# FFN weight sums made beside the float64 conversion and read back from DRAM, a group's second transposes moved three products on, first FFN products issued sooner

## The chip, the cores and the metric

One core of a Trainium2 chip runs the whole program in one launch. The metric is the device time of an execution in microseconds (us); less is better. The engines are named as the profile names them: PE (matrix multiply; PEld is its weight load), DVE (vector), ACT (scalar), POOL (GpSimd), SP (the engine that issues most DMAs here). Each engine runs its own instructions in program order and waits at semaphores for the others.

## The reference

Three stages follow each other, all in float32: an attention with exponential features, a mixture of eight experts with one expert for each token, and a dense feed-forward layer (FFN) with three parallel first matrices.

```python
def phi(x):
    proj = np.einsum('bhsd,df->bhsf', x, w_phi)
    proj = proj - np.max(np.abs(proj), axis=-1, keepdims=True)
    return np.concatenate([np.exp(proj), np.exp(-proj)], axis=-1)
q_p, k_p = phi(q), phi(k)                          # 8 batches, 8 heads, 576 tokens
kv = np.einsum('bhsf,bhsd->bhfd', k_p, v); z = np.sum(k_p, axis=2)
num = np.einsum('bhsf,bhfd->bhsd', q_p, kv)
x = num / (np.einsum('bhsf,bhf->bhs', q_p, z)[..., None] + 1e-06)   # -> (4608, 512)

do_compute = x @ w_skip > 0                        # the other tokens pass unchanged
e_idx = np.argmax(xc @ w_gate, axis=1)             # xc: the tokens computed
y[mask] = gate_w[mask, None] * (np.maximum(xc[mask] @ w1[e], 0) @ w2[e])
x[do_compute] = xc + y

h = np.maximum(np.maximum(x @ w1, x @ w2), x @ w3) # 512 -> 768, three matrices
out = h @ w_out                                    # 768 -> 512
```

## The kernel before

**Precision.** A float32 operand of a large product is split into a high part, made by a copy on ACT, and a low part, made by a subtraction on DVE. A product is then three matmuls (`mm3`, L483 to L485). A "split" below is such a pair of one ACT and one DVE instruction, 512 or 256 columns wide. The same lines, L795 and L796, do it for weights (tiles `w`, `wB`, `wC`) and for the FFN's input (tiles `xB`, `xT`).

**Attention** takes the first 360 us or so. Beside it runs `conv`, a generator that turns the 24 FFN weight tiles from float64 bits into float32: a load `pf`, four DVE steps and two ACT squares or copies `sq`, two POOL instructions (L202, L203), and a DMA of the result `da` to the DRAM tensor `wfd`. One of its steps is taken in each of 60 attention iterations, the rest by `pump`.

**Experts.** Blocks of up to three token tiles go through layer 1 and layer 2. `pump` stands after each part of a layer and does three things: it splits one or two expert weight tiles (`w_split`, loads five splits ahead by `w_dma`), or, when those are done, takes a step of `w1_prep`, and then a step of `conv`. POOL also issues the gathers of tokens (`xg`), the scatters of results (`xb<-y`, L966) and the index lists (L301). SP issues the loads `stg<-in_w_exp` and the stores to `wfd` in one order.

**FFN.** Each of the products is done by a seven-product scheme in place of eight: from the four quarters of an operand (x11, x12, x21, x22) four sums are made, and seven products of quarters or sums give the result. `Quad.step(p)` issues product p (six matmuls in layer 1). Products 1, 6, 5 and 3 accumulate in one PSUM tile, and after 1, 6 and 5 ACT copies the running value out (`pu`, L1124) before the next of them may start. DVE adds the results (L1109, L1111, L1112, L1134).

The 4608 tokens go in nine groups of 512. A group has nine quads in layer 1 (nine pairs of weight tiles) and two in layer 2. All groups do layer 1 first. `do(n, at, f)` hangs a piece of side work behind product `at` of quad n, in the order 6, 4, 1, 5, 7, 2, 3.

For its input a group needs two times eight transposes on PE (`f_xt`, L1060) into two PSUM tiles of the pool `ps_t` (`tp`), which then feed the splits `x_put` and the sums `x_sums` (DVE, L1075). The two halves (i = 0 and 1) use the same two PSUM tiles, one half after the other, so that the second half's transposes wait for the last read of the first half. `x_next` puts the halves at quads n0+5 and n0+6.

The weights of layer 1 come from `w1_steps`: for each of nine pairs it loads both tiles of `wfd` into one staging tile `stg` (four of them, shared with the expert loads and with `f_load`), makes four sums on POOL (`sc`, L799 to L802), and splits one half tile, one tile and two pairs of sums. The first three pairs are split during the last expert block, the others beside the first group's first quads, five steps a pair.

At the start of the FFN the first group's transposes, splits and sums are written out in full ahead of the first product.

Of the kernel before, what the change touches and what calls it, by code (L numbers as in the profile page):

```python
# [19 lines left out]
P = 128  # L20
# [25 lines left out]
def kernel(  # L46
# [43 lines left out]
    wfd = dram.tile([NFT, P, 512], F32, name="wfd")  # L90

# [89 lines left out]
    def from_double(t, pool, i):  # L181
# [23 lines left out]
        yield  # L205
        nc.sync.dma_start(out=wfd[i], in_=af)

    conv_done = [0]

    def conv_steps(pool):  # L210
        def start(i):
            t = pool.tile([P, 1024], I32, name="pf")
            nc.sync.dma_start(out=t, in_=w_ffn[i].bitcast(I32))
            return t

        nxt = start(0)
# [552 lines left out]
    sc_p = ctx.enter_context(tc.tile_pool(name="sc", bufs=2))  # L769
# [28 lines left out]
    def sums_left(sc, x11, x12, x21, x22, eng):  # L798
        eng.tensor_tensor(out=sc[:, 2], in0=x21, in1=x22, op=ALU.add)  # L799
        eng.tensor_tensor(out=sc[:, 0], in0=sc[:, 2], in1=x11, op=ALU.subtract)  # L800
        eng.tensor_tensor(out=sc[:, 1], in0=x11, in1=x21, op=ALU.subtract)
        eng.tensor_tensor(out=sc[:, 3], in0=x12, in1=sc[:, 0], op=ALU.subtract)  # L802

    def sums_right(sc, x11, x12, x21, x22, eng):
        eng.tensor_tensor(out=sc[:, 2], in0=x12, in1=x11, op=ALU.subtract)
        eng.tensor_tensor(out=sc[:, 0], in0=x22, in1=sc[:, 2], op=ALU.subtract)
        eng.tensor_tensor(out=sc[:, 1], in0=x22, in1=x12, op=ALU.subtract)
        eng.tensor_tensor(out=sc[:, 3], in0=x21, in1=sc[:, 0], op=ALU.subtract)

# [12 lines left out]
    class Operands:  # L822


        def __init__(self, raw, side, whole, half, sums, eng=nc.vector):
            self.raw, self.side, self.whole, self.half, self.pool, self.eng = raw, side, whole, half, sums, eng
            self.blocks = {}

        def steps(self):
            return [self.sums, self.single, self.wide, lambda: self.pair(0), lambda: self.pair(2)]  # L830

        def sums(self):
            r = self.raw
            x = [[r[:, a, b * 256 : (b + 1) * 256] for b in range(2)] for a in range(2)]
            self.sc = self.pool.tile([P, 4, 256], F32, name="sc")
            if self.side == "rows":
                sums_left(self.sc, x[0][0], x[0][1], x[1][0], x[1][1], nc.gpsimd)
            elif self.side == "cols":
                sums_left(self.sc, x[0][0], x[1][0], x[0][1], x[1][1], nc.gpsimd)
            else:  # L840
                sums_right(self.sc, x[0][0], x[0][1], x[1][0], x[1][1], nc.gpsimd)

        def single(self):
            h = self.half()
            rows = self.side == "rows"
            split(h, self.raw[:, 1, 256:] if rows else self.raw[:, 0, 0:256], self.eng)
            self.blocks[4 if rows else 1] = h

        def wide(self):
            w = self.whole()  # L850
            split(w, self.raw[:, 0 if self.side == "rows" else 1], self.eng)
            a, b = {"rows": (1, 2), "cols": (2, 4), "right": (2, 3)}[self.side]
            self.blocks[a], self.blocks[b] = w[:, :, 0:256], w[:, :, 256:]

        def pair(self, c):
            w = self.whole()
            split(w, self.sc[:, c : c + 2].rearrange("p a b -> p (a b)"))
            a, b = (6, 7) if c == 0 else (5, 4) if self.side == "right" else (5, 3)
            self.blocks[a], self.blocks[b] = w[:, :, 0:256], w[:, :, 256:]
# [10 lines left out]
    def w1_steps():  # L870
        half = halves(w1_tile)

        def load(p):
            while conv_done[0] < 2 * p + 2:
                next(conv)
            t = stg_p.tile([P, 2, 512], F32, name="stg")
            nc.sync.dma_start(out=t, in_=wfd[2 * p : 2 * p + 2].rearrange("i p c -> p i c"))
            return Operands(t, "rows", w1_tile, half, sc_p)

        cur, nxt = load(0), None  # L880
        yield
        cur.sums()
        for p in range(9):
            nxt = load(p + 1) if p < 8 else None
            yield
            while w1_used[0] + 4 > (freed[0] - WF + NWA + NWB if not wc_p else NWA + NWB + NWC + 4):
                yield
            for f in cur.steps()[1:]:
                f()
                yield  # L890
                if f == cur.wide and nxt:
                    nxt.sums()
            w1[p] = cur.blocks
            cur = nxt
# [142 lines left out]
    pu_p = fc.enter_context(tc.tile_pool(name="pu", bufs=5))  # L1037
    fx = ExitStack()
# [34 lines left out]
    def x_sums(g, i, part=(0, 1)):  # L1073
        a, b = xps[g, i], xps[g, i + 2]
        sub = lambda o, x, y: nc.vector.tensor_tensor(out=o, in0=x, in1=y, op=ALU.subtract)  # L1075
        if 0 in part:
            if g == groups[0]:
                sc = mt_p.tile([P, 2, 512], F32, name="mt").rearrange("p a (b c) -> p (a b) c", b=2)
            else:
                sc = sc_p.tile([P, 4, 256], F32, name="sc")  # L1080
            xsc[g, i] = sc
# [111 lines left out]
    def w2_load(k):  # L1193
        raw = stg_p.tile([P, 2, 512], F32, name="stg")
        nc.sync.dma_start(out=raw, in_=wfd[18 + k : 24 : 3].rearrange("i p c -> p i c"))
        op = Operands(raw, "right", lambda: wb_p.tile([P, 2, 512], F32R, name="wB"), w2_half, sc_p)
        w2[k], w2_op[k] = op.blocks, op.steps()
# [13 lines left out]
    def h_load(g, k, pool, name, sums):  # L1211
        raw = pool[0].tile([P, 2, 512], F32, name=name)
        nc.sync.dma_start(out=raw, in_=hd[g].rearrange("p (s f) t -> p f s t", s=2)[:, k])
        op = Operands(raw, "cols", h_tile, h_half, None)

        def with_pool():
            op.pool = sums[0]
            op.sums()

        hs[g, k], h_op[g, k] = op.blocks, [with_pool] + op.steps()[1:]  # L1220
# [20 lines left out]

    def op_step(ops, key, i):
        ops[key][i]()

    def to_layer2(n0):
# [3 lines left out]
        for k, (ld, at) in enumerate(((2, 6), (4, 1), (4, 1))):  # L1249
            do(n0 + ld, at, w2_load, k)  # L1250
# [7 lines left out]
        for k, plan in enumerate((  # L1258
# [6 lines left out]
        for k in range(3):  # L1265
            do(n0 + 7, 1, h_load, g1, k, stg, "stg", sb_p)
# [19 lines left out]

    g0 = groups[0]
# [173 lines left out]
```

## Time and profile before

| | |
|---|---|
| median of three runs | 1252.28 us (1249.16 to 1254.79) |
| the profiled execution | 1259.92 us |
| its span in the trace | 1258.0 us |
| granted TensorE clock, mean | 0.965 of full |

The profile and the views of the trace tell of the one profiled execution, which took 0.6% longer than the median. Times in the trace are counted from the start of its span.

### The profile page before, as it was taken

To read this page: it belongs to the slowest core of one execution; us is meant where nothing else is said; L and a number is where in the kernel's file an instruction comes from. 1 tells how busy PE (TensorE), PEld (TensorE's weight loads), DVE (VectorE), ACT (ScalarE), POOL (GpSimd) and SP (SyncE) were. 2 spreads that over 40 slices of the span, in tenths; PEclk is the share of its full clock that TensorE was granted. 3 is DMA by queue.
4 is the path that set the end of the run, shared out by engine and by line. 5 is a ranking of instruction groups with operands and counts; after the bars stand their busy time and mean duration, and the time that the engine had idled before them with its cause. 6 is when DMAs were issued, how large, how long until landed. Compare 5 with 4: busy or idle time off the path is not lost.

```text
span 1258.0 us, 34053 instructions
## 1 busy us (share of the span) xinstructions
PE 1138.3 (90%) x14212; PEld 1061.6 (84%) x14212; DVE 858.8 (68%) x1820; ACT 563.4 (45%) x1290; POOL 323.2 (26%) x358
## 2 busy tenths in 40 slices
PE   6998898899669699979997899999999999999996
PEld 5887777777568488959886899999999999999996
DVE  6888678778545177869878756556566566887772
ACT  4655454555443144556545333233233233455552
POOL 0001221221442346444245200000000000569770
PEclk9999999999987799989998999999999999999999
DMA  7566846855862366667744220110111111345541
GB/s 260 197 194 211 205 144 199 211 185 168 160 130 65 79 231 205 229 225 241 222 162 126 68 68 34 68 66 36 63 45 50 63 42 61 135 151 184 181 157 69
DMA packets 115470, 175.84 MB, mean 140 GB/s; under 512 B 20930, under 2 KB 58306, under 8 KB 115312
## 3 DMA queue, kind: packets, MB, share of 16 engines
q1 hardware_dynamic: 110592, 163.63, 41.8%
q0 software_dynamic: 4352, 8.71, 2.0%
q8 instruction: 113, 1.85, 0.6%
q10 hardware_dynamic: 368, 1.27, 0.3%
q14 instruction: 45, 0.37, 0.1%
HBM read 120.77 MB, written 54.78 MB: 140 GB/s over the span
## 4 chain that ended last, share of the span: by engine, by line
PE 68%; DMA 9%; DVE 7%; issue 7%; POOL 5%; ACT 2%; SPq 0%; POOLq 0%; ACTq 0%; DVEq 0%
PE mm L485 15%; PE mm L483 15%; PE mm L484 15%; PE kv L590 6%; PE n L630 6%; PE pr L550 6%; PE tr L567 3%; DMA list<-ids,idx 2%; PE n L608 1%; DMA xb<-y,ixr 1%; DMA xb<-y,ix0a 1%; PE tp L1060 1%; DVE sc L1075 1%; POOL sq L202 1%; POOL da L203 1%
## 5 line engine op out<-in xcount | busy, mean ns | idle before, releaser
L1124 ACT ACTIVATE pu<-mm 128x256 f32<-128x256 f32 x297 | 114.3, 385 | 270.9 <-PE mm L485 261.3
L1111 DVE TENSOR_TENSOR pu<-mm,pu 128x256 f32<-128x256 f32 x162 | 68.0, 420 | 95.2 <-PE mm L485 92.3
L799 POOL TENSOR_TENSOR sc<-stg 128x256 f32<-128x256 f32 x15 | 12.4, 823 | 408.6 <-DMA stg<-hd 374.9
L590 PE MATMUL kv<-raw,e 128*64 128x74 f32 (+1 forms) x2560 | 99.1, 234 | 12.5 <-issue 12.3
L630 PE MATMUL n<-kvw,q 128*64 128x74 f32 x2304 | 98.7, 237 | 12.3 <-issue 11.1
L590 PEld LDWEIGHTS kv<-raw,e 128*64 128x64 f32 (+1 forms) x2560 | 84.5, 137 | 28.7 <-issue 27.2
L576 ACT ACTIVATE e<-d 128x512 f32<-128x512 f32 x144 | 82.6, 621 | 49.0 <-DVE d L557 45.8
L555 DVE TENSOR_REDUCE m<-pr 128x8 f32<-128x1024 f32 x72 | 87.7, 1217 | 21.4 <-PE pr L550 10.9
L630 PEld LDWEIGHTS n<-kvw,q 128*64 128x64 f32 x2304 | 87.7, 143 | 16.2 <-issue 13.6
L550 PE MATMUL pr<-wph,raw 64*64 64x128 f32 x2304 | 87.0, 287 | 15.3 <-issue 8.7
L202 POOL TENSOR_TENSOR sq<-sq,pf 128x512 f32<-128x512 f32 x24 | 31.8, 1323 | 238.3 <-DVE pf L200 196.8
L557 DVE TENSOR_TENSOR d<-pr,m 128x1024 f32<-128x1024 f32 x72 | 88.2, 1224 | 4.9 <-ACT sq L185 0.5
L483 PE MATMUL mm<-xT,w 128*128 128x256 f32 x288 | 81.8, 284 | 9.1 <-ACT pu L1124 4.7
L569 ACT ACTIVATE q<-tr 128x512 f32<-128x512 f32 x72 | 42.8, 595 | 103.6 <-PE tr L567 95.2
L550 PEld LDWEIGHTS pr<-wph,raw 64*64 64x64 f32 x2304 | 67.6, 139 | 22.2 <-issue 16.4
L1109 DVE TENSOR_TENSOR mt<-mm,pu 128x256 f32<-128x256 f32 x135 | 56.2, 416 | 39.1 <-PE mm L485 38.6
L484 PE MATMUL mm<-xT,w 128*128 128x256 f32 x288 | 81.4, 282 | 0.0
L485 PE MATMUL mm<-xT,w 128*128 128x256 f32 x288 | 81.3, 282 | 0.0
L1112 DVE TENSOR_TENSOR mt<-mt,pu 128x256 f32<-128x256 f32 x162 | 71.7, 443 | 5.6
L484 PE MATMUL mm<-wB,w 128*128 128x256 f32 x266 | 74.6, 280 | 0.0
L485 PE MATMUL mm<-wB,w 128*128 128x256 f32 x266 | 74.5, 280 | 0.0
L483 PE MATMUL mm<-wB,w 128*128 128x256 f32 x266 | 74.4, 280 | 0.0
(278 smaller groups left out, 3813.3 us busy)
## 6 DMA issues: line engine op xcount, KB each, us to landing
raw<-in_qkv_dram SPq DMA_DIRECT2D x46, 798.0 KB
stg<-in_w_exp_dram SPq DMA_DIRECT2D x64, 512.0 KB
hd<-mt SPq DMA_DIRECT2D x27, 512.0 KB
pf<-in_w_ffn_dram SPq DMA_DIRECT2D x24, 512.0 KB
hb<-hd SPq DMA_DIRECT2D x21, 512.0 KB
xa<-xs SPq DMA_DIRECT2D x16, 576.0 KB
xb<-xs SPq DMA_DIRECT2D x16, 576.0 KB
stg<-xb SPq DMA_DIRECT2D x18, 512.0 KB
```

Of the source, the lines that this page charges most:

```text
L483: nc.tensor.matmul(out=ps, lhsT=ah, rhs=bh, start=first, stop=False, skip_group_check=on)
L484: nc.tensor.matmul(out=ps, lhsT=ah, rhs=bl, start=False, stop=False, skip_group_check=on)
L485: nc.tensor.matmul(out=ps, lhsT=al, rhs=bh, start=False, stop=last, skip_group_check=on)
L550: nc.tensor.matmul(out=pr[p0 : p0 + 64, h, 2 * s + i], lhsT=raw[k0, o + p0 : o + p0 + 64], rhs=wph[k0], start=True, stop=True,)
L555: nc.vector.tensor_reduce(out=m, in_=pr, axis=AX.X, op=ALU.max, apply_absolute_value=True)
L557: nc.vector.tensor_tensor(out=d, in0=pr, in1=m[:, :, :, None].to_broadcast([P, 2, 4, P]), op=ALU.subtract)
L576: nc.scalar.activation(out=e[:, :, :, s], in_=ds[s2][:, :, 2:4], func=AF.Exp, scale=scale)
L590: nc.tensor.matmul(out=kvps[u, b][c : c + 64, 2 * h + s], lhsT=e[p0:p1, h, i, s, c : c + 64], rhs=v[p0:p1, h], start=t == 4 * b and h + s ...
L630: nc.tensor.matmul(out=ps[p0 : p0 + 64, i, h], lhsT=q[:, s, 2 * h + i, p0 : p0 + 64], rhs=kvw[u, b][:, 2 * h + s], start=s == 0, stop=s == 1,)
L1111: nc.vector.tensor_tensor(out=tmp, in0=ps, in1=tmp, op=ALU.add)
L1112: nc.vector.tensor_tensor(out=out, in0=out, in1=tmp, op=ALU.max)
L1124: nc.scalar.activation(out=t, in_=ps, func=AF.Copy)
```

## The change

1. **Sums beside the conversion.** When the second tile of a pair is converted, POOL makes the four sums from the two results that are still on the chip, and they are stored in a new DRAM tensor `wsm`. `from_double` loses one of its steps and a pair gains two, so that a pair still has twelve.
2. **Weights loaded with their sums.** `Operands` no longer makes sums. Each pair is loaded in two parts into a staging tile each: one pair of sums (256 KB) with a whole tile (256 KB), then the other pair of sums (256 KB) with half a tile (128 KB). A pair is still three wide splits and one half split. The same holds for the three pairs of the last matrix (`w2`), whose tiles are laid out in another order in the input. The hidden operands of layer 2 keep their sums on POOL (`HiddenOperands`).
3. **Steps beside the first quads.** The steps of `w1_prep` hang behind all seven products of eight quads, one each, where they hung behind those of five quads.
4. **Second transposes.** A group's second half starts ten products after the first, and not seven; its splits and sums go with it.
5. **First products.** Products 1 and 2 of the first quad are issued between the first and the second eight transposes of the first group, product 6 and the next quad's product 1 ahead of the remaining splits. The first group's sums get tiles of their own (`sc`) in place of borrowed ones (`mt`), and the pool `sc` is opened in the FFN.

```diff
+    wsm = dram.tile([NFT // 2, P, 2, 512], F32, name="wsm")
...
-    def from_double(t, pool, i):
+    def from_double(t, pool, i, pair):
...
         nc.gpsimd.tensor_tensor(out=sq, in0=sq, in1=hi.bitcast(F32), op=ALU.mult)
         nc.gpsimd.tensor_tensor(out=af, in0=af, in1=sq, op=ALU.add)
         yield
-        yield
         nc.sync.dma_start(out=wfd[i], in_=af)
+        pair.append(af)
...
         for i in range(NFT):
             t, nxt = nxt, start(i + 1) if i + 1 < NFT else None
             yield
-            yield from from_double(t, pool, i)
-            conv_done[0] = i + 1
+            yield from from_double(t, pool, i, pair)
+            if i % 2:
+                yield
+                x = [v[:, c : c + 256] for v in pair for c in (0, 256)]
+                sm = pool.tile([P, 4, 256], F32, name="sm", bufs=1)
+                (sums_left if i < 18 else sums_right)(sm, *x, nc.gpsimd)
+                pair.clear()
+                yield
+                nc.sync.dma_start(out=wsm[i // 2], in_=sm.rearrange("p (a b) c -> p a (b c)", a=2))
+                conv_done[0] = i // 2 + 1
...
+        def load(self, n, p):
+            right = self.side == "right"
+            t = stg_p.tile([P, 2, 512], F32, name="stg")
+            nc.sync.dma_start(out=t[:, 1 - n] if n == 0 else t[:, 0], in_=wsm[p, :, n])
+            if n == 0:
+                nc.sync.dma_start(out=t[:, 0], in_=wfd[2 * p + right])
+            elif right:
+                nc.sync.dma_start(out=t[:, 1, 0:256], in_=wfd[2 * p, :, 0:256])
+            else:
+                nc.sync.dma_start(out=t[:, 1, 0:256], in_=wfd[2 * p + 1, :, 256:])
...
+        def step(self, i):
+            right = self.side == "right"
+            if i == 3:
+                h = self.half()
+                split(h, self.src[3])
+                self.blocks[1 if right else 4] = h
+            else:
+                w = self.whole()
+                split(w, self.src[i])
...
         for i in range(2):
-            q = n0 + 5 + i
-            do(q, 0, f_ps, g, i)
-            do(q, 0, f_xt, g, i)
-            for at, p in ((2, 1), (3, 2), (4, 3)):
-                do(q, at, x_put, g, p, i)
-            do(q, 5, x_sums, g, i, (0,))
-            do(q, 6, x_sums, g, i, (1,))
+            q = 7 * (n0 + 5) + 10 * i
+            at = [divmod(q + t, 7) for t in range(8)]
+            do(*at[0], f_ps, g, i)
+            do(*at[0], f_xt, g, i)
+            for t, p in ((2, 1), (3, 2), (4, 3)):
+                do(*at[t], x_put, g, p, i)
+            do(*at[5], x_sums, g, i, (0,))
+            do(*at[6], x_sums, g, i, (1,))
...
             for p in (1, 2):
                 for i in range(2):
                     x_put(g0, p, i)
+            step(0, 1)
+            step(0, 2)
     for i in range(2):
         x_sums(g0, i, (0,))
     for i in range(2):
         x_put(g0, 6, i)
+    step(0, 6)
     for i in range(2):
         x_sums(g0, i, (1,))
+    step(1, 1)
...
-    for n in range(5):
+    for n in range(8):
         for at in range(7):
             do(n, at, next, w1_prep, None)
-    do(5, 0, list, w1_prep)
```

The first place is PE's order at the start of the FFN (`stg` holds the group's tokens; `tp` and `mm` are PSUM tiles). Before:

```order
1806 L1060 MATMUL tp<-ident,stg 128x128 x4
1807 L1060 MATMUL mm<-ident,stg 128x128 x4
1808 L1060 MATMUL tp<-ident,stg 128x128 x4
1809 L1060 MATMUL mm<-ident,stg 128x128 x4
1810 L483 MATMUL mm<-xB,w 128x256
```

Now:

```order
1806 L1085 MATMUL tp<-ident,stg 128x128 x4
1807 L1085 MATMUL mm<-ident,stg 128x128 x4
1808 L505 MATMUL mm<-xB,w 128x256
...
1819 L507 MATMUL mm<-xB,w 128x256
1820 L1085 MATMUL tp<-ident,stg 128x128 x4
1821 L1085 MATMUL mm<-ident,stg 128x128 x4
1822 L505 MATMUL mm<-xT,w 128x256
```

Rows 1808 to 1819 are the twelve matmuls of products 1 and 2, which stood behind the second eight transposes and now stand ahead of them.

The second place is DVE's order in a later group, at the second half's first splits (`xB<-tp`) and sums (`sc`), among the adds of products. Before:

```order
988 L1075 TENSOR_TENSOR sc<-tp,sc 128x256 x2
989 L1111 TENSOR_TENSOR pu<-mm,pu 128x256
990 L1112 TENSOR_TENSOR mt<-mt,pu 128x256
991 L796 TENSOR_TENSOR xB<-tp,xB 128x256 x2
992 L1109 TENSOR_TENSOR mt<-mm,pu 128x256
```

Now:

```order
983 L1100 TENSOR_TENSOR sc<-tp,sc 128x256 x2
984 L1132 TENSOR_TENSOR pu<-mm,pu 128x256
985 L1133 TENSOR_TENSOR mt<-mt,pu 128x256
986 L1130 TENSOR_TENSOR mt<-mm,pu 128x256
987 L1132 TENSOR_TENSOR pu<-mm,pu 128x256
988 L1133 TENSOR_TENSOR mt<-mt,pu 128x256
989 L817 TENSOR_TENSOR xB<-tp,xB 128x256 x3
```

Between the last read of the first half (`sc<-tp,sc x2`) and the first split of the second half three more adds of products stand now.

The third place is POOL's order late in the expert stage, around a scatter (`xb<-y`). Before:

```order
165 L202 TENSOR_TENSOR sq<-sq,pf 128x512
166 L203 TENSOR_TENSOR da<-da,sq 128x512
167 L202 TENSOR_TENSOR sq<-sq,pf 128x512
168 L203 TENSOR_TENSOR da<-da,sq 128x512
169 L966 DMA xb<-y,ixr_7568 4608x512 x2
170 L464 MEMSET xg 128x528
```

Now:

```order
211 L203 TENSOR_TENSOR sq<-sq,pf 128x512
212 L204 TENSOR_TENSOR da<-da,sq 128x512
213 L217 TENSOR_TENSOR sm<-da 128x256
214 L218 TENSOR_TENSOR sm<-da,sm 128x256
215 L219 TENSOR_TENSOR sm<-da 128x256
216 L220 TENSOR_TENSOR sm<-da,sm 128x256
217 L990 DMA xb<-y,ixr_7614 4608x512 x2
```

The four sums of a pair now stand between the second tile's conversion and the next scatters and gathers. Of the twelve pairs five lie in the attention, seven in the expert stage.

## Rows read from the trace of the kernel before

**Rows 1.** The page: busy time and share of PE, weight loads, DVE, ACT, POOL.

```profile
PE 1138.3 (90%) x14212; PEld 1061.6 (84%) x14212; DVE 858.8 (68%) x1820; ACT 563.4 (45%) x1290; POOL 323.2 (26%) x358
```

**Rows 2.** Stretches: length, busy time of each engine, PE clock, DMA share, GB/s.

```profile
430.00:661.00 231.00, 215.56 (x1300) 188.75 (x1300) 175.78 (x304) 117.06 (x238) 102.12 (x111) 0.95 0.66 217
661.00:722.00 61.00, 48.50 (x355) 46.63 (x354) 49.88 (x103) 29.78 (x77) 22.25 (x26) 0.89 0.32 99
722.00:1053.00 331.00, 322.67 (x2708) 319.99 (x2707) 195.01 (x500) 112.00 (x314) 0.00 (x0) 1.00 0.16 55
```

**Rows 3.** PE's waits from 660 us on: total us, times, longest.

```profile
PE tp L1060 <- DVE sc L1075: 9.5, 16, 1.0
PE mm L483 <- ACT pu L1124: 4.7, 1, 4.7
PE mm L483 <- DVE pu L1111: 4.1, 2, 3.4
```

**Rows 4.** Timeline of PE in the fourth group: start, us, [idle before].

```profile
761.47 0.63 PE L1060 MATMUL tp<-ident,stg 128*128 128x128 f32 x4 [0.24 <-DVE sc L1075]
763.05 0.63 PE L1060 MATMUL tp<-ident,stg 128*128 128x128 f32 x4 [0.95 <-DVE sc L1075]
```

**Rows 5.** Timeline of PE at the start of the FFN.

```profile
664.97 1.45 PE L1060 MATMUL tp<-ident,stg 128*128 128x128 f32 x4 [0.28 <-DVE xB L796]
666.22 1.06 PE L1060 MATMUL mm<-ident,stg 128*128 128x128 f32 x4
673.95 0.58 PE L483 MATMUL mm<-xT,w 128*128 128x256 f32 x1 [4.66 <-ACT pu L1124]
679.36 0.28 PE L483 MATMUL mm<-xB,w 128*128 128x256 f32 x1
679.48 0.28 PE L484 MATMUL mm<-xB,w 128*128 128x256 f32 x1
```

**Rows 6.** Timeline of ACT in the same place.

```profile
669.68 1.33 ACT L795 ACTIVATE xT<-mt 128x256 fp32r<-128x256 f32 x4 [2.40 <-DMA xb<-y,ixr]
673.51 0.38 ACT L1124 ACTIVATE pu<-mm 128x256 f32<-128x256 f32 x1
```

**Rows 7.** Timeline of PE around the second long wait.

```profile
694.65 0.39 PE L483 MATMUL mm<-xT,w 128*128 128x256 f32 x1 [3.39 <-DVE pu L1111]
696.06 0.41 PE L484 MATMUL mm<-xB,wB 128*128 128x256 f32 x1
696.27 0.41 PE L485 MATMUL mm<-xB,wB 128*128 128x256 f32 x1
```

**Rows 8.** Two short stretches, columns as in rows 2.

```profile
690.00:700.00 10.00, 6.61 (x43) 6.41 (x42) 9.90 (x17) 3.73 (x9) 6.69 (x8) 0.83 0.02 4
661.00:664.00 3.00, 0.64 (x6) 0.40 (x5) 2.70 (x4) 1.05 (x2) 2.92 (x3) 1.00 0.83 305
```

**Rows 9.** DVE instructions of lines L171, L557 and L796: ns min/median/max.

```profile
L171 DVE TENSOR_TENSOR w<-stg,w x59: 669/692/1798, 460.5 to 645.7; 128x512 fp32r<-128x512 f32 x59
L557 DVE TENSOR_TENSOR d<-pr,m x72: 1223/1224/1225, 9.9 to 363.4; 128x1024 f32<-128x1024 f32 x72
L796 DVE TENSOR_TENSOR xT<-mt,xT x8: 410/415/426, 670.1 to 674.7; 128x256 fp32r<-128x256 f32 x8
```

**Rows 10.** The first and last of POOL's four sums: count, busy us, mean ns.

```profile
L802 POOL TENSOR_TENSOR sc<-stg,sc 128x256 f32<-128x256 f32 x15 | 15.2, 1010 | 0.0
L799 POOL TENSOR_TENSOR sc<-stg 128x256 f32<-128x256 f32 x15 | 12.4, 823 | 408.6 <-DMA stg<-hd 374.9 <-DVE wB L796 14.6 <-PE mm L485 9.6
```

**Rows 11.** Waits of ACT and of SP's queue, 425 to 640 us.

```profile
ACT sq L185 <- POOL da L203: 20.1, 11, 5.7
ACT w L169 <- DMA stg<-in_w_exp_dram: 15.1, 11, 3.8
...
SPq L206 <- POOL da L203: 94.5, 14, 12.7
```

**Rows 12.** The chain that ended last, at the FFN's start: start us, us, what.

```profile
659.78 3.72 DMA stg<-xb
```

More of the change, by code (lines that the diff above doesn't have):

```diff
@@ L214, in start @@
             return t
-        nxt = start(0)
+        nxt, pair = start(0), []
         for i in range(NFT):
@@ L822, with __init__ @@
     class Operands:
[L825 to L832, printed above, removed]
+        def __init__(self, side, whole, half):
+            self.side, self.whole, self.half, self.blocks = side, whole, half, {}
@@ L843, in single @@
[L843 to L859, printed above, removed]
+            elif i == 1:
+                h = self.half()
+                split(h, r[:, 0, 0:256])
+                self.blocks[1] = h
+            else:
+                w = self.whole()
+                src = r[:, 1] if i == 2 else self.sc[:, 2 * i - 6 : 2 * i - 4].rearrange("p a b -> p (a b)")
+                split(w, src)
+                a, b = ((2, 4), (6, 7), (5, 3))[i - 2]
+                self.blocks[a], self.blocks[b] = w[:, :, 0:256], w[:, :, 256:]
@@ L871, in w1_steps, with load @@
         half = halves(w1_tile)
[L873 to L880, printed above, removed]
+        ops = [Operands("left", w1_tile, half) for _ in range(9)]
+        def load(n):
+            p, part = divmod(n, 2)
+            if p < 9:
+                while conv_done[0] <= p:
+                    next(conv)
+                ops[p].load(part, p)
+        load(0)
         yield
-        cur.sums()
         for p in range(9):
[L884 to L894, printed above, removed]
+            for part in range(2):
+                load(2 * p + part + 1)
+                if part == 0:
+                    while w1_used[0] + 4 > (freed[0] - WF + NWA + NWB if not wc_p else NWA + NWB + NWC + 4):
+                        yield
+                for i in (2 * part, 2 * part + 1):
+                    ops[p].step(i)
+                    yield
+            w1[p] = ops[p].blocks
     w1_prep = w1_steps()
@@ L1076, in x_sums @@
         if 0 in part:
[L1077 to L1081, printed above, removed]
+            sc = xsc[g, i] = sc_p.tile([P, 4, 256], F32, name="sc")
             nc.scalar.activation(out=sc[:, 3], in_=a[:, 256:], func=AF.Copy)
@@ L1191 @@
     w2_op = {}
[L1193 to L1197, printed above, removed]
+    for k in range(3):
+        w2_op[k] = Operands("right", lambda: wb_p.tile([P, 2, 512], F32R, name="wB"), w2_half)
+        w2[k] = w2_op[k].blocks
     h_used = [0]
@@ L1240, in x_next, with w2_load @@
             do(n0 + 9, 2 + i, x_put, g, 4, i)
+    def w2_load(k, part):
+        w2_op[k].load(part, 9 + k)
     def op_step(ops, key, i):
-        ops[key][i]()
+        ops[key].step(i)
     def to_layer2(n0):
@@ L1285, in h_next, with step @@
                     do(*at[first + k], op_step, h_op, (g, k), s)
+    quads = [(quad1, g, p) for g in groups for p in range(9)] + [(quad2, g, m) for g in groups for m in range(2)]
+    made = {}
+    def step(n, p):
+        if 0 <= n < len(quads):
+            if n not in made:
+                f, *args = quads[n]
+                made[n] = f(*args)
+            made[n].step(p)
     g0 = groups[0]
@@ L1406 @@
             for f in range(6):
-                nc.tensor.matmul(out=ps, lhsT=hm[:, f], rhs=f_weight(18 + f), start=f == 0, stop=f == 5)
+                nc.tensor.matmul(out=ps, lhsT=hm[:, f], rhs=f_weight(18 + 2 * (f % 3) + f // 3), start=f == 0, stop=f == 5)
             o = ov_p.tile([P, DM], F32, name="oo")
```

71 lines of the change are left out of this document (33 added, 38 removed), and 6 rows, old and new, of tables (at, q).

## The prediction

> **What bounds the kernel now.** The page first: PE is busy 90% of the span and nothing else above 84%, and that one is PE's own weight load [rows 1]. So what counts is where PE stands still, or runs at the lower of its two clocks. The busy times by stretch show three regimes [rows 2]. In the middle of the FFN, 722 to 1053 us, PE is busy 322.67 of 331 us at full clock. At its start, 661 to 722 us, it is busy 48.5 of 61 us, with 0.89 of the clock. In the expert stage, 430 to 661 us, it is busy 215.56 of 231, DVE 175.78 and POOL 102.12. Then PE's waits in the FFN [rows 3]: 9.5 us in 16 waits of transposes for DVE's sums, one of 4.7 us for an ACT copy and 4.1 us in two for a DVE add, 18.3 us in all. So a change there can bring some 20 us and not much more, slow clock included. A change in the expert stage can only cost, unless it takes work from DVE or POOL.
>
> **The second transposes.** The second eight transposes of a later group come in two pieces, which waited 0.24 and 0.95 us [rows 4]. They write the two PSUM tiles that DVE is still reading for the sums of the first half. The 16 waits of [rows 3] are eight groups with two each, 9.5 / 8 = 1.19 us a group. Three products are 18 matmuls, at full clock 0.12 us apart (679.36 and 679.48 in [rows 5]), so the transposes come 2.1 us later against a wait of 1.19 us. DVE gets three adds of products in between, but the read that PE waits for stands ahead of those. The second half's splits of sums for product 6 are not moved and lie five products behind the moved sums, so nothing is late next. The term is -9.5 us; its bounds are -9.5 and 0 (the wait comes back for another reason).
>
> **The first products.** PE stood still for 4.66 us and went on at 673.95, when ACT had made the copy of product 1 [rows 5]. That copy ran at 673.51 [rows 6], though product 1 was done before: it stood in ACT's order behind all the splits of the input. These in turn began at 669.68, after 2.40 us of waiting for a scatter, because the tile they write lies where the scattered result lay. Now the copy stands behind the first splits. In exchange the second eight transposes come behind products 1 and 2. The new path, step by step: product 1 can start when the transposes did that wait for the same split, at 664.97; twelve matmuls at the slow clock, 0.21 us apart (696.06 and 696.27 in [rows 7]), end at 667.5; eight transposes, four of which took 1.06 us, end at 669.6; then an ACT copy (0.38), two DVE subtractions and the low part of a split (0.42 each) and ACT's high part, put as long as the copy [rows 6, 9], 2.0 us. Product 6 starts at 671.6 in place of 673.95. The scatter that held the splits back is the last of its kind and stood on POOL behind eight sums, which are gone. The term is -2.35 us; bounds -4.7 (the whole wait) and 0.
>
> **Weights beside the first quads.** The second stop, 3.39 us at 694.65, waited for an add that stood behind weight splits on DVE [rows 7]; from 690 to 700 us DVE was busy 9.90 of 10 us while POOL made sums for 6.69 [rows 8]. A split of 512 columns takes 692 ns in the median and up to 1798 [rows 9]; I put the long ones down to POOL's sums, since DVE's instruction that reads PSUM, and runs beside POOL all through the attention, never leaves 1223 to 1225 ns.
>
> The Trainium skill's page "SBUF — State Buffer", section "Who interferes with whom", says that a DVE instruction with two SBUF inputs is held up by a GpSimd instruction that reads SBUF, and one with at most one SBUF input is not. By it the 20 sums moved into the attention would cost the PSUM readers nothing, and the 28 in the expert stage could hold up its splits; the spread of [rows 9] agrees.
>
> So the 36 sums that leave the FFN's start make DVE faster there. Three of the wide splits also go ahead of the first product. But the rest now come seven to a quad, where they came in five steps a pair with one of them a load. A quad is 42 matmuls, 5.0 us; seven splits (five wide at 0.69, two half at 0.42) are 4.3 us, and the adds of a quad six to seven instructions of 0.42, 2.7 us. That is 7.0 us of DVE against 5.0 of PE for three quads, 6 us of lag, of which six PSUM accumulators hide about one quad's chain. The staging also moves 896 KB a pair in place of 512. At the 305 GB/s that [rows 8] show in the busiest stretch, the nine parts left (4.0 MB) take 13 us against some 15.5 us for their 22 steps; only the first of them, which waits for a staging tile, should hold ACT up, by about the 3.72 us that a load took to land [rows 12]. I take -1.5 us: part of the 3.4 us is saved. Bounds: -6.9 (the stop, and 3.5 us for the slow clock behind both stops, which has doubled the distance of the matmuls at 696.06 and is gone at 679.36 [rows 5, 7]: up to 5 us at half speed behind the first and some 2 behind the second) and +3.
>
> **Sums in the expert stage.** Four sums take 0.82 to 1.01 us each, 3.7 us together [rows 10].  Seven pairs are 26 us more of POOL in 231 us, of which it used 102 [rows 2]. Room there is, but three orders tighten. ACT waits for POOL's conversion already, 20.1 us in 11 waits, and the next tile's square now comes one `pump` sooner. DVE's first step for the next pair needs a buffer that the sums still read. And SP stands 94.5 us in 14 waits at its stores of converted tiles with the expert loads queued behind them [rows 11]; the store of the sums adds a stop of up to 3.7 us for each pair. Loads go out five splits ahead, so most of it is hidden. DVE has 55 us to spare in the stage, and PE holds several accumulators. I take +3 us, near the lower end, because none of PE's long waits in this stage is for these three. Bounds 0 and +26 (every sum in full).
>
> **At nothing.** In the attention the sums are spread over 60 iterations; where its last pair meets the index scatters, whose DMAs wait for one another, the conversion ahead of it comes one step sooner as the sums come later: 0, bounds -3 and +3.7 (four sums in front of the last scatters). For the last matrix twelve sums leave POOL and its loads have several products to land: 0, bounds -1 and +1.
>
> **The sum.** -9.5 - 2.35 - 1.5 + 3 = -10.35 us on an execution of 1259.92, whose span is 1258.0; 1249.6, a ratio of 0.9918. The profiled execution stands 0.6% above the median of 1252.28, so the forecast for the median is 1242.
>
> **The rivals.**
> - *More is won.* The expert stage hides all, and both stops go with their slow clock: -9.5 - 4.7 - 6.9 = -21.1, some 1231. For it: DVE's splits were half as long again beside POOL. Against it: 7.0 us of DVE to a quad.
> - *The start gives back.* Loads and splits of weights keep ACT and DVE late as before (0 and +1), and the expert stage costs 7: -1.5, some 1251. What decides is whether a part lands within three steps, 2.1 us, of its use. The Trainium skill's page "DMA: Bandwidth & Descriptors", section "Bandwidth", speaks for it: it asks for transfers of 1 MiB or more and shows smaller ones at lower rates, and these shrink from 512 to 256 and 128 KB; no run here shows the smaller ones yet.
> - *The wait moves along.* The second transposes find another reason to wait for 1.19 us: -0.85, some 1251. For it only that DVE's adds stand in between.
> - *Slower.* SP's new stops at the stores of sums use up the lead of the expert loads, ACT stands in its splits, and layer 1's results come late: all 26 us in place of 3 give +12.7, some 1265. It needs more than 19.6 us of the 26 to be slower by 0.5%. For it: SP's 94.5 us. Against it: ACT's waits for these loads are 15.1 us in 11 and hardly one reaches PE.
>
> **How the numbers follow.** The forecast has 0.47 (1237 to 1248), more won 0.18, the start gives back 0.20, the wait that moves 0.06, slower 0.09. A measurement of this kernel can tell about 0.5%, 6.3 us, from no change. Below 1246 lie the forecast but for 0.04, all of the second and 0.06 of the third: 0.67. Above 1258.5 lies 0.09. The rest is 0.24. The range leaves out the lower half of the first rival and the slower case: 1232 to 1255.
>
> **What would show it.** Right: no PE wait for `sc` at the transposes; product 6 of the first quad at some 2 to 3 us less behind the last expert matmul; POOL idle from 665 to 1050 us; a stop of at most 3 us in the first four quads; the stretch from the attention's end to the last expert matmul 0 to 6 us longer. Wrong: PE waiting for `ht` or `xt` in the expert stage for 5 us more than now, ACT waiting for `stg<-wsm` for several us beside the first quads, or the transposes still waiting.

## The result, and the profile after

The changed kernel took 1268.85 us in the median of four runs (1262.28 to 1272.22), beside 1252.57 for the kernel before: a ratio of 1.0107 (95% interval 1.0072 to 1.0142). It is 1.1% slower; 1242 had been forecast. Beside a later set of kernels it was 1.0135 (1.0100 to 1.0170). All ratios leave out two executions of this study that took over 1.5% longer than the fastest of their kernel.

The profiled execution took 1262.28 us, the shortest of its four, while that of before, 1259.92, was longer than any of its timed runs; so the two spans, 1260.4 and 1258.0, hide most of the difference, and the kernels are compared stage by stage. The **stage** below means the time from the first to the last expert matmul, the **rest** the time from there to the end of the span.

The page of the changed kernel, busy times as in [rows 1]:

```profile
PE 1142.0 (91%) x14212; PEld 1063.0 (84%) x14212; DVE 848.1 (67%) x1820; ACT 561.9 (45%) x1290; POOL 318.5 (25%) x358
```

No engine is much busier. The stretches tell more; columns as in [rows 2]. First the stage in the kernel before:

```profile
392.00:661.00 269.00, 244.31 (x1464) 214.75 (x1461) 190.08 (x351) 122.07 (x249) 112.86 (x123) 0.94 0.59 191
```

Then the changed kernel's stage, its start of the FFN and the middle of it:

```profile
386.00:679.00 293.00, 254.60 (x1456) 218.25 (x1455) 190.55 (x357) 123.17 (x253) 126.76 (x139) 0.93 0.60 196
679.00:735.00 56.00, 47.22 (x346) 45.35 (x347) 37.65 (x91) 26.62 (x71) 0.97 (x1) 0.91 0.42 135
735.00:1053.00 318.00, 318.00 (x2689) 318.00 (x2688) 193.01 (x496) 111.77 (x313) 0.00 (x0) 1.00 0.17 57
```

In the middle of the FFN PE no longer waits at all, and at its start POOL is all but idle. But the stage grew from 269.0 to 292.6 us, exactly from the first to the last matmul: PE stood still for 38.4 us in place of 24.7, and was busy with the same matmuls for 10.3 us more, at a granted clock of 0.93 against 0.94. In slices of 1 us, busy time times the missing share of the clock adds up to 13.8 us in place of 7.9, so by this estimate the clock makes some 6 of the 10.3 us; where the other 4 come from is not shown. The rest fell from 596.7 to 581.9 us. So +23.6 and -14.9; the attention ahead of them began the stage at 386.0 and 392.3 us in these two executions, and anywhere from 378 to 399 in all other profiles of this study but one (412.1).

PE's waits in the FFN of the changed kernel, from 679 us on; what was [rows 3]:

```profile
PE tp L1085 <- DMA stg<-xb: 5.3, 2, 4.9
PE mm L505 <- ACT xT L816: 2.0, 2, 1.2
PE mm L505 <- ACT pu L1145: 1.2, 2, 0.6
```

The 16 waits for the sums are gone, and so are the stops of 4.7 and 3.4 us. What answers to [rows 5], the first group's transposes and product 6 (the last expert matmul ended at 678.5):

```profile
683.45 0.74 PE L1085 MATMUL tp<-ident,stg 128*128 128x128 f32 x4 [4.92 <-DMA stg<-xb]
...
689.63 0.38 PE L505 MATMUL mm<-xT,w 128*128 128x256 f32 x1 [1.25 <-ACT xT L816]
```

Product 6 starts 11.1 us behind the last expert matmul; before it was 12.7 (673.95 in [rows 5] and 661.27).

In the stage, 386 to 679 us, PE waits for what ACT and DVE have to make for it:

```profile
PE tp L512 <- DMA xg<-xa,ixr: 10.9, 2, 10.2
PE mm L968 <- ACT y L961: 7.8, 2, 5.8
PE mm L507 <- DVE ht L497: 7.1, 11, 2.1
PE mm L506 <- DVE xt L501: 6.1, 3, 2.7
PE mm L505 <- ACT ht L495: 4.7, 5, 2.7
PE mm L507 <- DVE xt L501: 1.4, 1, 1.4
```

The waits for `ht` and `xt` are 19.3 us; before they were 4.7 (the prediction's sign of being wrong was 5 us more). ACT's, DVE's and SP's waits in the same stretch, to be held against [rows 11]:

```profile
ACT w L170 <- DMA stg<-in_w_exp_dram: 31.5, 12, 5.0
ACT sq L186 <- POOL da L204: 29.5, 10, 7.5
...
ACT wB L170 <- DMA stg<-in_w_exp_dram: 10.4, 5, 3.1
```

```profile
DVE da L188 <- POOL sm L214: 11.3, 3, 6.0
```

```profile
SPq L206 <- POOL da L204: 105.8, 14, 14.3
...
SPq L242 <- POOL sm L214: 8.5, 4, 2.9
SPq L242 <- POOL sm L220: 8.3, 3, 3.1
```

Directly or by way of SP, these are waits for POOL: ACT's square for the conversion of the tile before (20.1 us in [rows 11]), DVE for the sums, SP at the stores, and behind SP the expert loads, for which ACT waits 41.9 us in its splits (19.3 before, of it 15.1 in [rows 11]). POOL in its turn waits at its scatters, most of it for layer 2's results `y` (count | busy us, mean ns | idle us before, and for what):

```profile
L990 POOL DMA_INDIRECT xb<-y,ixr x16 | 19.5, 1217 | 81.4 <-DVE y L984 67.8 <-DVE ht L497 7.0 <-DMA xb<-y,ixr 6.4
```

Its busy time in the stage rose by only 13.9 us (112.86 to 126.76): 28 sums came, and the 12 for the first three pairs, which had stood at the stage's end, went. The stage grew by more than that.

One place shows how it comes about. POOL, then ACT, then PE of the changed kernel; a number in brackets is the idle time ahead:

```profile
516.62 1.07 POOL L211 TENSOR_TENSOR sm<-da 128x256 f32<-128x256 f32 x1
...
519.13 1.19 POOL L214 TENSOR_TENSOR sm<-da,sm 128x256 f32<-128x256 f32 x1
520.49 1.33 POOL L990 DMA_INDIRECT xb<-y,ixr  x1 [0.16 <-issue]
528.18 1.00 POOL L990 DMA_INDIRECT xb<-y,ixr  x1 [6.37 <-DMA xb<-y,ixr]
...
531.54 1.30 POOL L203 TENSOR_TENSOR sq<-sq,pf 128x512 f32<-128x512 f32 x1
532.91 1.26 POOL L204 TENSOR_TENSOR da<-da,sq 128x512 f32<-128x512 f32 x1
```

```profile
534.21 0.66 ACT L186 ACTIVATE sq<-pf 128x512 f32<-128x512 f32 x1 [4.36 <-POOL da L204]
534.77 0.37 ACT L495 ACTIVATE ht<-mm 128x256 fp32r<-128x256 f32 x1
```

```profile
535.19 0.50 PE L505 MATMUL mm<-wB,ht 128*128 128x512 f32 x1 [2.66 <-ACT ht L495]
```

At this place the sums stand ahead of the first scatter, the second scatter waits for the first to land, the conversion stands behind both, ACT's square behind the conversion, layer 1's eviction behind the square, and PE behind that.

### The profile page after: what moved, and what is told of

The parts are those of the page before. It is cut to its first block, busy times and chain, and to the rows that moved or that the text cites. A ratio compares the mean times of both kernels' runs of the same rounds, so it can differ in the third digit from the quotient of the medians.

```text
span 1260.4 us, 34159 instructions
## 1 busy us (share of the span) xinstructions
PE 1142.0 (91%) x14212; PEld 1063.0 (84%) x14212; DVE 848.1 (67%) x1820; ACT 561.9 (45%) x1290; POOL 318.5 (25%) x358
## 4 chain that ended last, share of the span: by engine, by line
PE 50%; DVE 4%; DMA 3%; issue 2%; POOL 1%; ACT 1%; SPq 0%; POOLq 0%; DVEq 0%; ACTq 0%
PE mm L507 16%; PE mm L506 16%; PE mm L505 16%; PE tp L1085 1%; DMA xb<-y,ixr 1%; DMA stg<-xb 1%; DVE w L817 1%; DVE w L172 1%; DMA ltr<-list 0%; DVE wB L172 0%; POOL sq L203 0%; POOL da L204 0%; DMA stg<-in_w_exp_dram 0%; DMA stg<-wfd 0%; PE tp L512 0%
## 5 line engine op out<-in xcount | busy, mean ns | idle before, releaser
L211 POOL TENSOR_TENSOR sc<-stg 128x256 f32<-128x256 f32 x6 | 5.1, 844 | 427.7 <-DMA stg<-hd 397.7
L652 PE MATMUL n<-kvw,q 128*64 128x74 f32 x2304 | 95.8, 235 | 11.8 <-issue 9.9
L505 PE MATMUL mm<-xT,w 128*128 128x256 f32 x324 | 92.6, 286 | 3.4 <-ACT xT L816 2.0
L506 PE MATMUL mm<-xT,w 128*128 128x256 f32 x324 | 91.9, 284 | 0.4 <-DVE xT L817 0.4
L507 PE MATMUL mm<-xT,w 128*128 128x256 f32 x324 | 91.5, 282 | 0.0
```

The source lines that it names most:

```text
L505: nc.tensor.matmul(out=ps, lhsT=ah, rhs=bh, start=first, stop=False, skip_group_check=on)
L506: nc.tensor.matmul(out=ps, lhsT=ah, rhs=bl, start=False, stop=False, skip_group_check=on)
L507: nc.tensor.matmul(out=ps, lhsT=al, rhs=bh, start=False, stop=last, skip_group_check=on)
L652: nc.tensor.matmul(out=ps[p0 : p0 + 64, i, h], lhsT=q[:, s, 2 * h + i, p0 : p0 + 64], rhs=kvw[u, b][:, 2 * h + s], start=s == 0, stop=s == 1,)
```

## Experiments

All numbers of stage and rest come from the timeline of PE in one profiled execution each; ratios are to the kernel before on the same chip, over all executions. The two profiled executions of the changed kernel have stages that differ by 3.3 us, so a smaller difference of two stages says nothing. Where ratio and stage tell different stories, the text gives both.

| kernel | stage us | rest us | ratio (95% interval) |
|---|---|---|---|
| before | 269.0 | 596.7 | 1 |
| changed | 292.6 | 581.9 | 1.0107 (1.0072 to 1.0142) |
| changed, again | 295.9 | 582.2 | 1.0135 (1.0100 to 1.0170) |
| moves alone | 271.2 | 585.5 | 0.9859 (0.9833 to 0.9885) |
| spacing alone | 284.6 | 598.0 | 1.0124 (1.0091 to 1.0157) |
| changed, no sums | 288.1 | 582.8 | 1.0063 (1.0033 to 1.0094) |
| old spacing | 293.1 | 581.2 | 1.0033 (1.0004 to 1.0063) |
| old spacing, no sums | 274.9 | 581.4 | one run, no ratio |
| late stores | 293.1 | 581.5 | 1.0058 (1.0038 to 1.0078) |
| two squares | 283.7 | 581.9 | 1.0001 (0.9968 to 1.0034) |
| old spacing, two squares | 282.0 | 582.8 | 0.9951 (0.9927 to 0.9976) |
| two squares, late stores | 278.7 | 582.7 | 0.9933 (0.9896 to 0.9970) |
| old spacing, conversion on DVE | 262.3 | 582.6 | 0.9811 (0.9761 to 0.9862) |
| the same, sums on DVE | 260.6 | 583.4 | 0.9793 (0.9735 to 0.9850) |
| moves, conversion on DVE | 258.3 | 584.0 | 0.9780 (0.9735 to 0.9825) |
| changed, early conversion | 258.8 | 582.4 | 0.9886 (0.9825 to 0.9946) |

**The moves alone.** The kernel before with parts 4 and 5; the add of product 2 stays behind the splits, where `mt` is free.

```diff
+            step(0, 1)
+            step(0, 2, late)
...
+    step(0, 6)
...
+    step(1, 1)
...
+            q = 7 * (n0 + 5) + 10 * i
```

> The kernel before with parts 4 and 5 of the change alone: the second transposes three products on, products 1, 2 and 6 of the first quad and product 1 of the second issued sooner (the add of product 2 stays where it was). No sums in DRAM. Theory S (the sums beside the conversion cost the 23.6 us by which the expert stage, first to last expert matmul, grew from 269.0 to 292.6 us; the moves are worth what was forecast): expert stage 268 to 271 us, no wait for the sums at the transposes, 9 to 13 us faster than before, about 1241. Rival R (the moves themselves upset the FFN, and the transposes' wait only comes out elsewhere): within 4 us of before.

Theory S held for the moves: stage 271.2 us, and 1.4% faster. That is some 17 us, more than the 9 to 13 expected; stage and rest of the two profiled executions hold 9.0 of it. PE's waits from 660 us on in this kernel:

```profile
PE mm L483 <- DVE pu L1111: 4.1, 2, 3.4
...
PE mm L483 <- DVE mt L1109: 2.6, 2, 2.0
```

The transposes' wait is gone; the second stop stays as in [rows 3], and DVE's adds are late by 1.6 us more than before.

**What in the conversion costs.** First the sums left out of the changed kernel, then its spacing alone put into the kernel before, then the sums with the old spacing, then that without sums.

```diff
+        sm = pool.tile([P, 4, 256], F32, name="sm", bufs=1)
+        nc.gpsimd.memset(sm, 0.0)
...
-                (sums_left if i < 18 else sums_right)(sm, *x, nc.gpsimd)
```

> The changed kernel without the four sums on POOL of each pair: a tile of zeros is stored in their place, so the order of all steps, the stores and the traffic are those of the changed kernel, and the FFN weights' sums are zero. Theory S1 (the sums' own time on POOL, and those who wait for POOL: the next pair's DVE step, ACT's square, SP's store of the sums): the expert stage falls from 292.6 to 275 us or less. Rival S2 (not the sums but the conversion step taken one sooner, and more stores in SP's order): it stays above 285 us. Rival S3 (DVE held up by POOL's sums): as S1, and the DVE splits in the stage get shorter by over 5%.

288.1 us: the sums' absence brings back 4.5 us only, so S2 seemed right. S3 fell: DVE's splits into `w` and `wB` took 817 and 728 ns in the mean, against 811 and 755 in the changed kernel.

```diff
         yield
-        yield
         nc.sync.dma_start(out=wfd[i], in_=af)
...
+            if i % 2:
+                yield
+                yield
```

> The kernel before with the conversion's steps spaced as in the changed kernel: one step less behind POOL's two instructions of each tile, two empty steps behind each second tile. No sums, no new stores. Theory S2 (the spacing: the next tile's square on ACT and the store on SP come one step sooner behind POOL, which without the sums on POOL still left 288.1 us of expert stage): expert stage 280 us or more, against 269.0 to 271.2 with the old spacing; slower than before by 0.6% to 1.2%. Rival D (the 512 KB of sums stored for each pair and the steps that they take in SP's order): stage below 273 us, time within 0.4% of before.

284.6 us: the spacing alone, with no sum and no new store, costs 13 to 16 us, and by the ratio 1.24%, just above the range expected.

```diff
+        yield
+        if i % 2:
...
+            (sums_left if i < 18 else sums_right)(sm, *x, nc.gpsimd)
+            pair[:] = [sm]
         yield
         nc.sync.dma_start(out=wfd[i], in_=af)
```

> The changed kernel with the conversion spaced as before: six steps a tile; a pair's sums run on POOL in the step between the second tile's conversion and its store, the sums are stored one step into the next tile. Same instructions, stores and traffic. Theory S2: expert stage 270 to 276 us (the sums' own 4.5 us left), FFN 582 us as in the changed kernel; 10 to 16 us faster than before. Rival D: the stage stays above 282 us.

S2 fell: with the old spacing the stage is as long as ever, 293.1 us, and the kernel is not faster than before (1.0033). The time did fall, though: 1.0033 stands beside 1.0135 for the changed kernel in the same set of runs, 12 to 13 us less. Of this, in the two profiled executions, 6.6 us lie ahead of the first expert matmul (392.3 against 398.9 us), 2.9 in the stage and 1.0 in the rest. So the spacing may cost something ahead of the stage too; how is open. The next run left the sums out of this one.

```diff
-            (sums_left if i < 18 else sums_right)(sm, *x, nc.gpsimd)
-            pair[:] = [sm]
+            pair[:] = [zeros[0]]
```

> The changed kernel with the old spacing of the conversion, and without POOL's sums: a tile of zeros is stored in their place. With the old spacing and with sums the expert stage took 293.1 us; without sums and stores 269.0 to 271.2. Theory T (the sums' time on POOL, which lies ahead of scatters, gathers and the next conversion in POOL's order, costs the 22 us): stage 270 to 276 us. Rival D (the stores of the sums, in SP's order and as traffic): 286 us or more.

274.9 us, as T expects, in a single execution. So by these stages, with the old spacing, the stores cost 4 to 6 us (from 269.0 and 271.2) and the sums 18 more. With the new spacing, which costs 13 to 16 us by itself, stores and sums add 3.5 and 4.5 (284.6, 288.1, 292.6). In the stages of these executions sums and spacing each make the stage long, and both together hardly longer than one of them, as two ways to run into one obstacle would. The ratios speak against that: by them the spacing costs 1.24% alone and 1.0% with stores and sums in place (1.0033 and 1.0135), so there it nearly adds up. Which of the two holds is open.

**By which wait it reaches PE.**

```diff
-        nc.sync.dma_start(out=wfd[i], in_=af)
+        stores.append([3, wfd[i], af, None])
```

> The changed kernel with the stores of converted tiles and of sums issued two conversion steps later; nothing else moved. Theory P (SP stands at these stores, 105.8 and 16.8 us, expert loads queue behind them, and ACT waits for the loads: 41.9 us in 17 waits against 19.3 in 14 before): SP's waits at the stores fall below 50 us, ACT's waits for expert loads below 20, the expert stage by 12 us or more, to 280 or less. Rival A (ACT and DVE wait for POOL itself, not for loads): SP's waits fall as much, the stage by 5 us at most.

In the stage nothing came back: 293.1 us. The ratio, 1.0058, is below the changed kernel's 1.0107 and 1.0135, by 6 to 10 us; the profiled execution was the longest of its ten. ACT's waits in this kernel:

```profile
ACT sq L186 <- POOL da L204: 43.1, 11, 8.5
...
ACT w L170 <- DMA stg<-in_w_exp_dram: 8.7, 5, 3.8
```

ACT's waits for loads went (12.8 us with `wB`, from 41.9), and its wait for POOL grew from 29.5 to 43.1: by the stage this is Rival A, while by the ratio part of the loss came back, though less than the 12 us of Theory P. Part of SP's stop moved to the load of the next tile, whose buffer POOL still reads (65.9 us).

```diff
-        sq = pool.tile([P, 512], F32, name="sq", bufs=1)
+        sq = pool.tile([P, 512], F32, name="sq", bufs=2)
```

> The changed kernel with two buffers in place of one for the tile that ACT's square fills and POOL reads. Theory A (ACT's square waits for POOL's conversion of the tile before, 29.5 us in 10 waits against 20.1 in 11 before, and the expert splits and the evictions of layer 1 stand behind it): that wait goes, the expert stage falls by 10 us or more, to 282 or less. Rival P (loads behind SP's stores): the stage falls by 4 us at most, because ACT then waits for the loads.

8.9 us came back, nearly the 10 of Theory A (by the ratios 13 to 17), and the other wait grew; ACT here:

```profile
ACT w L170 <- DMA stg<-in_w_exp_dram: 40.3, 18, 7.2
...
ACT wB L170 <- DMA stg<-in_w_exp_dram: 15.5, 7, 5.3
```

55.8 us for loads in place of 41.9. With the old spacing the second buffer brought 11 us:

> The kernel spaced as before and with two buffers for the tile of ACT's square. Theory S2 with A (ACT's square behind POOL is what the spacing makes late): expert stage 264 to 272 us, no more than 4 us below the one with one buffer, since the wait is then mostly gone already. If the two are independent costs, it is 8 to 9 us below the one with one buffer (two buffers brought 8.9 us in the changed kernel).

282.0 us, not the 264 to 272 of S2 with A: what the second buffer brings does not hang on the spacing. Both together, the second buffer and the late stores:

> The changed kernel with both: two buffers for the tile of ACT's square (alone: expert stage 283.7 us), and SP's stores two conversion steps later (alone: 293.1). POOL's order and time are as in the changed kernel. Theory W (the loss reaches PE by two ways side by side, ACT's square and SP's stores with the loads behind them, and each carries it when the other is closed): stage 274 us or less. Rival G (it reaches PE by something else behind POOL, as the gathers of the next block's tokens or DVE's wait for the sums): stage 281 us or more.

278.7 us lies between the two expectations: closing both ways gives back 14 of the 21 us that the changed kernel has over the moves alone. ACT still waits 32.9 us for loads. Of the remaining 7 us, PE's waits for `ht` and `xt` make 3.5 (10.0 against 6.5), those for gathered tokens and for `y` 2.4 (23.5 against 21.1); what lies behind them is open.

**Taking the conversion out of POOL's order.**

```diff
-        nc.gpsimd.tensor_tensor(out=sq, in0=sq, in1=hi.bitcast(F32), op=ALU.mult)
-        nc.gpsimd.tensor_tensor(out=af, in0=af, in1=sq, op=ALU.add)
+        if i >= 10:
+            yield
+        eng = nc.vector if i >= 10 else nc.gpsimd
+        eng.tensor_tensor(out=sq, in0=sq, in1=hi.bitcast(F32), op=ALU.mult)
+        eng.tensor_tensor(out=af, in0=af, in1=sq, op=ALU.add)
```

> The changed kernel with the old spacing, and in the expert stage the two instructions of each tile's conversion that ran on POOL now on DVE, one step later; the sums stay on POOL. Theory Q (the loss comes through POOL's one order: scatters that wait for layer 2's results stand ahead of the conversion, the sums ahead of the scatters, and ACT's square, SP's stores and the expert loads behind the conversion): ACT's and SP's waits for POOL go, expert stage 276 us or less in place of 293.1. Rival V (DVE is as short of time: 14 tiles by two instructions of 0.69 us are 19 us more on it): 285 us or more.

262.3 us, as Theory Q expects: with the sums still on POOL, 31 us of stage went, more than the change had cost. ACT's square now waits 4.5 us, in place of 28.6 with the conversion on POOL and the old spacing. But SP still stands 69.5 us at the stores of converted tiles (96.6), now for DVE, and ACT waits for the expert loads as long as before (27.4 and 28.8 us): the 31 us did not come by the loads. The stage of this kernel, columns as in [rows 2]:

```profile
378.00:640.00 262.00, 240.48 (x1460) 212.44 (x1456) 195.95 (x384) 123.61 (x253) 91.09 (x111) 0.97 0.67 219
```

> The kernel with the moves alone (stage 271.2 us, 1.4% faster than before), and the conversion's two POOL instructions on DVE in the expert stage, one step later. Theory Q: ACT waits 24.4 us for POOL there, SP 96.4; the stage falls to 266 us or less, 1.6% or more faster than before. Rival V: the stage grows to 274 us or more.

258.3 us, as Theory Q expects, and the fastest of all, 2.2% ahead of the kernel before (its interval overlaps with those of the two others on DVE). So the same edit takes 13 us off a stage without the sums too. All three kernels on DVE also take the two instructions one conversion step later, and rid DVE's splits of POOL's company (last section); no run parts these from the queue. With the sums on DVE as well:

> The kernel with the conversion on DVE in the expert stage (stage 262.3 us) and the sums of its seven pairs on DVE too, 28 instructions of about 0.42 us, 12 us of DVE in place of 26 of POOL. If POOL's sums still hold up scatters and gathers: stage 256 to 260 us. If they are hidden and DVE's time is what counts: 264 us or more. Between them: no difference to be told.

No difference to be told: 260.6 against 262.3. And with the sums on POOL the stage is 4.0 us longer than with the moves alone on DVE, which is what the stores cost without any sums. So, as far as single stages can tell, POOL's sums cost about nothing once no conversion stands behind them.

```diff
                 next(conv)
+                next(conv)
```

> The changed kernel with two conversion steps in each attention iteration in place of one: ten pairs are converted beside the attention and two in the expert stage. All theories that put the loss on the conversion in the expert stage: that stage falls to 270 us or less. What it costs the attention is open: nothing by its spare time (DVE busy 273 of the first 360 us, ACT 186, POOL 75), up to 40 us if DMA traffic (0.67 of its share used) or DVE becomes its bound.

With ten pairs converted beside the attention the stage is 258.8 us, as short as with DVE, and here nothing changed its engine. The profiled execution is the longest of its kernel, 1255.24 us, and its first expert matmul came only at 412.1 us. What the attention pays is told by the ratio: 0.9886 where stage and rest save 24.5 us, 2%; about 10 us is given back (3 to 18 by the interval).

The changed kernel was run once more beside these:

> The changed kernel once more, beside the others. All theories: expert stage 290 to 295 us, 581 to 583 us from the last expert matmul to the end, slower than before by 0.5% to 1.3%.

It repeats, a little above what was expected: 295.9 and 582.2 us, slower by 1.35%.

## Why the prediction was wrong

**The failed step** is "I take +3 us, near the lower end, because none of PE's long waits in this stage is for these three". The term *sums in the expert stage* measures +23.6 us, and +26.9 the second time; its upper bound had been +26. The step before it, "Room there is", counted POOL's free time (102 of 231 us in [rows 2]), and the bound of 26 left out that 12 sums leave the stage. What counts is when POOL gets to the conversion: its two instructions stand behind scatters that wait for layer 2, and ACT's square and SP's stores stand behind them. The prediction named these waits (20.1 and 94.5 us in [rows 11]) and took most of them to be hidden. They were not: taking the conversion off POOL shortens the stage of the kernel with the moves alone from 271.2 to 258.3 us. There ACT and SP wait for DVE at the square and the stores:

```profile
ACT sq L185 <- DVE da L206: 5.2, 6, 1.5
```

```profile
SPq L210 <- DVE da L206: 42.7, 8, 6.5
SPq L210 <- DVE ht L479: 33.1, 5, 10.7
SPq L210 <- DVE da L187: 5.7, 1, 5.7
```

The square's wait fell from 24.4 us to 5.2, SP's stop at the stores only from 96.4 to 81.5. So SP's stop, the larger number, could stay; which share of the loss each wait carries is not shown further than by the runs above. That PE had no long wait for `ht` or `xt` did not say that there was slack.

- **Second transposes: right, mis-sized a little.** With the moves alone the wait of 9.5 us is gone, and from product 6 to the end it is 576.2 us in place of 584.1: -7.9 against the -9.5 forecast; DVE's adds are waited for 1.6 us more.
- **First products: right.** With the moves alone product 6 is 9.3 us behind the last expert matmul, 3.4 less than before (forecast 2.35). In the changed kernel it is 1.6, with the group's first load waited for 4.9 us in place of 2.4 (the load of [rows 12]); why that load comes later is not shown.
- **Weights beside the first quads: right in sign.** The rest is 3.6 us shorter than with the moves alone, against -1.5. From 679 us on ACT waits 3.4 us in all for the smaller loads, so the rival *the start gives back*, which rested on them, fell.
- **The FFN terms together** were -13.35 and measure -14.9.
- **At nothing:** the term for the attention is not settled. The first expert matmul lies within the spread of all the kernels, but with the old spacing it came 6.6 us sooner than in the changed kernel beside it, in one execution of each.
- **The rival "Slower"** named the place and nearly the size (1265), at a chance of 0.09. Its mechanism, SP's stops with the loads behind them, is one of two ways, and the lesser: late stores alone left the stage at 293.1 us (by the ratio 6 to 10 us came back); with ACT's square closed they brought 5 us (283.7 to 278.7).

The stage's +23.6 and the rest's -14.9 give +8.7 us, 0.7%, the second time +12.4, 1.0%; measured were 1.1 and 1.4%. Some 5 us of the loss thus lie in neither, and no run shows where. The sum of stage and rest stands within 0.7% of every ratio of the table but that of the early conversion, yet does not hit them; the attention of an execution spreads by more than that.

## What to carry to other kernels

An engine that is busy a quarter of the time can still set the pace, if other engines wait in their own order for something that stands behind a wait in its order: ask what is ahead of the instruction, not how much of the engine is free. Two rows of waits for one engine in several queues (here ACT's square and SP's stores for POOL) are the sign, even where PE shows no wait for them. Which of them counts, their size does not tell: SP's was the larger, and most of it stayed in the fastest kernel. Moving the two instructions to DVE, which makes one input of each, took 31 us off the stage with the sums and 13 off that with the moves alone. An edit that removes one of two such waits can move much of it to the other, so close both before calling either harmless. And a stage read from one execution is a weak witness: hold it against the times of all executions before building on a few us.

## What the runs showed of the hardware

The 0.69 us that a split of 512 columns takes on DVE is its time without POOL. The splits of expert weights in the changed kernel, ns min/median/max:

```profile
L172 DVE TENSOR_TENSOR w<-stg,w x59: 670/691/1816, 453.9 to 662.9; 128x512 fp32r<-128x512 f32 x59
L172 DVE TENSOR_TENSOR wB<-stg,wB x55: 668/684/1775, 393.3 to 660.5; 128x512 fp32r<-128x512 f32 x55
```

The same splits with the conversion and the sums on DVE:

```profile
L172 DVE TENSOR_TENSOR w<-stg,w x59: 669/682/694, 457.0 to 635.3; 128x512 fp32r<-128x512 f32 x59
L172 DVE TENSOR_TENSOR wB<-stg,wB x55: 668/684/694, 398.3 to 632.8; 128x512 fp32r<-128x512 f32 x55
```

With POOL's conversion and sums gone no split takes over 694 ns. So in the kernel with the moves alone DVE took on the 28 instructions of the conversion (0.69 us each, 19 us), yet was busy in the stage for 191.87 us in place of 189.51: its other instructions became shorter by almost as much. In the changed kernel POOL took 1.39 us for each of the two. The Trainium skill's page "SBUF — State Buffer", section "Who interferes with whom", says that a GpSimd instruction that reads SBUF holds up a DVE instruction with two SBUF inputs; these rows agree. The Trainium skill's page "GPSIMD Engine Reference", section "Engine selection", puts GpSimd at about twice DVE's time for such an instruction; 1.39 against 0.69 agrees.
